# The transform over the sequence in an attention, Fourier and MLP kernel: nine products over all outputs, or even and odd rows apart for half of them

## The chip, the cores and the metric

One Trainium2 chip; the kernel runs on one of its cores. Times are microseconds on the device; the time of a kernel is the median of its runs. Engines are named as in the profile: PE (matmuls; PEld is its weight load), DVE (vector), ACT (scalar), POOL (GpSimd), SP (which issues the DMAs).

## The reference

Three stages run one after the other on 4 batches of 576 rows and 512 features.

```
out_up    = repeat(softmax_attention(mean4(q), mean4(k), mean4(v)), 4)   # over groups of 4 rows
out_local = softmax_attention(q, k, v, only where |i - j| < 4)
x = out_up + out_local                                # [4, 576, 512], 8 heads of 64

mixed = real(fft(fft(x, over the 576 rows), over the 512 features))
u = x + mixed
ch = relu(layernorm(u) @ w_ch1) @ w_ch2               # 512 -> 2048 -> 512
x = u + ch

gate = sigmoid(causal depthwise convolution of x, 5 taps)
out = (gate * (x @ w_val)) @ w_out
```

The part at issue is `mixed`. The real part of the two Fourier transforms is a product with cosines over features and rows less a product with sines over both. Outputs m and 576 - m of the transform over the rows differ by the sign of the sine part alone, so 289 outputs of each part are computed (m = 0 to 288).

## The kernel before, in words

**Layout.** `X` of a batch holds 4 x 128 features on partitions and the 576 rows along the free dimension. All of `attn_steps(b)` (from L428) works on one batch: the local and the low-resolution attention, then the transform, which adds `mixed` to `X` in place. What follows works on units of 192 rows (`UT`), three a batch, twelve in all: `ln` (L1009) normalizes a unit, `mlp_steps` (L1133; `steps32`, L1095, for the first unit, in fp32) has the two big products, `moe2_steps` (L1189) the gated stage. Large products in fp16 are made of three matmuls each: both operands are split into a high and a low fp16 part, and the product of the low parts is left out.

**The transform of a batch** has these steps, from L842 on:

- *Folding* (L857 to L880): for c = 0, 1 (feature halves) and sd = 0, 1, DVE (POOL for sd = 1 of batches 1 to 3) makes `fs`, DVE makes `fF` by adding and subtracting row t and row 576 - t (289 rows kept, two parities e), ACT rounds it to `FH` in fp16 (L876), and DVE makes the rest `FL` (L877).
- *Transform over the features* (L891 to L917; L845 to L855 in batch 0, where it runs piece by piece after each fold): `TT` cuts the 289 rows into groups of 97, 96 and 96. The rows of a group are the weights' columns (`lhsT`), the moving operand is 127 to 129 columns of the table `feat`; 72 matmuls a batch fill `ab` in PSUM. ACT rounds it to `AH`, DVE makes `AL`, with the group's rows on partitions and 514 features along the free dimension.
- *Transform over the rows* (`seq_mm`, L919; `sums0`, L929, has the same loop for batch 0): for each c, `pp` (cosines) and `pq` (sines) are sums over the three groups and three fp16 passes: nine matmuls with 128 columns of `AH` or `AL` as weights and 289 columns of the table `seq` moving. `pn` is the same for the one feature 256 left over, with one column of weights. That makes five products a batch.
- *Sums* (L943 to L960; L970 to L987 for batches 1 to 3): ACT copies `pq` times a scale to `qs`; DVE makes `DS[:, 0]` = scaled `pp` - `qs` and `DS[:, 1]` = scaled `pp` + `qs`, the outputs 0 to 288 and those mirrored. ACT overwrites row 0 of `DS` of c = 0 with `pn`. Eight additions put `DS` on the two halves of `X`: 289 rows read forward, 287 read backward (`HALF - 2:0:-1`). For batches 1 to 3 the backward ones run on POOL. In batch 0 four of the eight read a mirrored copy in PSUM (`mir`).

`qs`, `DS`, `fs`, `fF` and other tiles of this kind share one ring of three buffers (tag "E" of `prp`). `pp`, `pq`, `pn` and `ab` share two banks of PSUM (tag "t", L35 to L39).

**Weights.** `w_ch1`, `w_ch2`, `w_val` and `w_out` come as 64-bit words; DVE makes fp32 of them by integer operations (`to_f32`, L303) in ring buffers, which the next loads reuse.

**Order.** The program is a list of events with positions in units of MLP stages: `spread` (L1371) puts a batch's steps between two positions (`P_D`, `P_E`, `S_F0`), `urgent` (L176) raises a step's priority (the transform has key "F"). Within that, the compiler of the kernel orders the instructions of each engine by priority and by a model of their costs, worked out anew at every build, gives out buffers of the rings and adds the waits; on the chip each engine runs its list strictly in order.

Of the kernel before, what the change touches and what calls it, by code (L numbers as in the profile page):

```python
# [25 lines left out]
HALF = S // 2 + 1  # L26
TT = ((0, 97), (97, 96), (193, 96))
SCALE = 0.125
# [67 lines left out]
def constants():  # L96
# [12 lines left out]
    wt[0] = wt[-1] = 0.5  # L109
    seq = np.zeros((97, 2, 3, 2, HALF))  # L110
    for j, m in enumerate((np.cos(ang) * wt, np.sin(ang) * (wt == 1.0))):
        for i, (n0, n) in enumerate(TT):
            seq[:n, j, i, 0] = m[n0:n0 + n]
    h, lo = split16(seq[:, :, :, 0])
    seq = np.stack([h, lo], 3)
    p, c = np.arange(128)[:, None], np.arange(128)[None, :]
# [6 lines left out]
        "c_feat": np.ascontiguousarray(feat.reshape(128, 2048)),  # L123
        "c_seq": np.ascontiguousarray(seq.reshape(97, 12 * HALF)),
        "c_band": (np.concatenate([band.reshape(128, 4 * WK), eye], 1).view(np.int32) >> 16).astype(np.int16),
# [5 lines left out]
def attn_moe_kernel(ctx, tc, q_t, k_t, v_t, w1, w2, w_val, conv_t, w_out, c_feat, c_seq, c_band, c_eye, out):  # L131
# [91 lines left out]
    def load_consts2():  # L223
        load(out=craw, in_=conv_t)
        load(out=feat, in_=c_feat.rearrange("p (a b c) -> p a b c", a=2, b=2))
        load(out=seq, in_=c_seq.rearrange("p (a b c d) -> p a b c d", a=2, b=3, c=2))

# [200 lines left out]
    def attn_steps(b):  # L428
# [414 lines left out]
        abs_ = []  # L843

        def piece(c, sd):  # L845
            if not abs_:
                abs_.extend(pst(x, [97, 512]) for x in ("ab", "ab", "eT"))
            for i, (n0, n) in enumerate(TT):
# [41 lines left out]

        for i, (n0, n) in enumerate(TT):  # L891
            def f(i=i, n0=n0, n=n):
                ps = abs_[i] if b == 0 else pst("ab", [97, 512])
                for (c0, c1), sd, e in () if b == 0 else [(FC[z], z % 2, z // 2) for z in range(4)]:
                    t = 0
                    for c in range(2):
                        for x, w in (("FH", 0), ("FH", 1), ("FL", 0)):
                            T.matmul(  # L898
                                out=ps[0:n, c0:c1], lhsT=d[x][:, c, sd, e, n0:n0 + n],
                                rhs=feat[:, w, c, c0:c1], start=(t == 0), stop=(t == 5),  # L900
                            )
                            t += 1
# [16 lines left out]
        def seq_mm(ps, col, m, j):  # L919
            t = 0  # L920
            for i, (n0, n) in enumerate(TT):
                for x, w in (("AH", 0), ("AH", 1), ("AL", 0)):
                    d["seqed"] = T.matmul(
                        out=ps, lhsT=d[x][0:n, i, col:col + m], rhs=seq[0:n, j, i, w, :],
                        start=(t == 0), stop=(t == 8),
                    )
                    t += 1

        def sums0():  # L929

# [24 lines left out]
            for e in (1, 0):  # L955
                A.activation(out=DSs[0][0:1, e], in_=pn, func=AF.Copy, scale=d["ivx8"][0:1, 0:1])
# [7 lines left out]
        for c in range(2 if b else 0):  # L964
            def f(c=c):
                pp = pst("pp", [P, HALF])
                seq_mm(pp, 128 * c, 128, 0)
                pq = pst("pq", [P, HALF])
                seq_mm(pq, 258 + 128 * c, 128, 1)
                qs = prp.tile([P, HALF], F32, tag="E", name="qs", bufs=3)  # L970
                iv = d["ivx8"][:, 0:1]
                A.activation(out=qs, in_=pq, func=AF.Copy, scale=iv)
                DS = prp.tile([P, 2, HALF], F32, tag="E", name="DS", bufs=3)
                stt(V, DS[:, 0], pp, iv, qs, ALU.mult, ALU.subtract)
                i = stt(V, DS[:, 1], pp, iv, qs, ALU.mult, ALU.add)
                X = d["X"]
# [506 lines left out]
```

## Time and profile before

| | |
|---|---|
| median of 3 runs | 725.42 us (724.97 to 728.31) |
| the profiled execution | 727.02 us |
| its span in the profile | 725.2 us |
| mean granted clock of PE, of full speed | 0.971 |

The span is the time from the profile's first to its last instruction; the rest of the execution's own time (1.8 us) lies around it. The clock of PE is at its full level outside 20 to 60 us and a stretch near 260 us. In the profile a matmul's busy time runs to its modelled end, and matmuls overlap; their pace is read from the chain of work or from their starts.

### The profile page before, as it was taken

Reading aid. Unit: us, or ns where it says so; the run is one execution under the profiler, and the core shown is the slowest. Engines: PE = TensorE matmul, PEld = TensorE weight load, DVE = VectorE, ACT = ScalarE, POOL = GpSimd, SP = SyncE. Lnnn points to the kernel's source line nnn. Section 1 sums busy time; section 2 is a strip of 40 time slices with the busy share of each in tenths; the row PEclk is TensorE's granted clock in tenths of the full one; section 3 lists DMA queues with packets and bytes.
Section 4 is the critical chain, followed back from the end, with each engine's and each line's share of the span. In section 5 each row is a group of like instructions: output and inputs, shape, how many; then the busy total and the mean of one; then the engine's idle time right before and its main releaser. Section 6 shows DMA issues by size and latency. Waiting matters only on the chain.

```text
span 725.2 us, 18322 instructions
## 1 busy us (share of the span) xinstructions
PE 680.2 (94%) x7785; PEld 591.6 (82%) x7785; DVE 462.7 (64%) x975; ACT 327.1 (45%) x999; POOL 118.6 (16%) x167
## 2 busy tenths in 40 slices
PE   8498798999989969999999999999999999999997
PEld 4265598898888749787998898798899989999895
DVE  4669699969885796628677625739535672723324
ACT  3574273796423465656434644834323232222222
POOL 2200012431120252330211316003100010000000
PEclk9659999999999989999999999999999999999999
DMA  8975352531435001240130001002000000000001
GB/s 243 295 285 177 117 208 67 140 126 33 145 99 154 17 2 36 99 116 17 45 120 3 20 21 43 16 12 89 15 17 15 2 16 16 2 16 2 31 1 45
DMA packets 27574, 53.01 MB, mean 73 GB/s; under 512 B 2112, under 2 KB 16320, under 8 KB 26468
## 3 DMA queue, kind: packets, MB, share of 16 engines
q1 hardware_dynamic: 27492, 51.84, 22.8%
q8 instruction: 61, 1.00, 0.6%
q14 instruction: 21, 0.17, 0.1%
HBM read 45.34 MB, written 8.26 MB: 74 GB/s over the span
## 4 chain that ended last, share of the span: by engine, by line
PE 62%; DVE 20%; DMA 9%; ACT 4%; POOL 2%; issue 2%; SPq 1%; ACTq 0%; DVEq 0%; POOLq 0%
PE pc L1166 18%; PE ph L1146 17%; DVE W L168 8%; PE out L1274 6%; PE val L1258 4%; DMA vw<-in_v_dram 2%; PE po L785 2%; PE pc L1121 2%; DMA v<-in_v_dram 2%; PE dO L617 2%; DMA raw<-in_moe_w_out_dram 1%; PE ab L898 1%; PE sc L734 1%; DVE qkT L628 1%; PE eT L775 1%
## 5 line engine op out<-in xcount | busy, mean ns | idle before, releaser
L1146 PE MATMUL ph<-uh,W 128*128 128x192 f16 x1408 | 197.0, 247 | 1.4 <-ACT uh L1072 1.4
L1146 PEld LDWEIGHTS <-W 128*128 128x128 f16 x2112 | 176.4, 98 | 10.3 <-issue 7.6
L1146 PE MATMUL ph<-ul,W 128*128 128x192 f16 x704 | 173.8, 247 | 0.0
L1166 PE MATMUL pc<-hh,W 128*128 128x192 f16 x1232 | 171.1, 246 | 0.0
L1166 PEld LDWEIGHTS <-W 128*128 128x128 f16 x1848 | 153.5, 98 | 5.5 <-issue 4.1
L1166 PE MATMUL pc<-hl,W 128*128 128x192 f16 x616 | 150.6, 246 | 1.3 <-DVE hl L168 1.3
L168 DVE SCALAR_TENSOR_TENSOR hl<-ph,hh 128x384 f16<-128x384 f32 x88 | 48.5, 552 | 90.5 <-ACT hh L1150 90.3
L1150 ACT ACTIVATE hh<-ph 128x384 f16<-128x384 f32 x88 | 43.1, 489 | 102.4 <-PE ph L1146 97.6
L168 DVE SCALAR_TENSOR_TENSOR W<-X,cw,W 128x192 f32<-128x192 f32 x160 | 60.7, 433 | 0.5 <-ACT W L1221 0.2
L1258 PE MATMUL val<-yy,W 128*128 128x192 f16 x576 | 53.2, 246 | 2.3 <-DVE yy L168 2.0
L1258 PEld LDWEIGHTS <-W 128*128 128x128 f16 x576 | 48.1, 98 | 4.4 <-issue 2.6
L576 ACT ACTIVATE dP<-dS,dmx 128x64 f32<-128x64 f32 x160 | 48.0, 333 | 3.3 <-PE dPT L597 2.6
L1274 PE MATMUL out<-W,gh 128*128 128x512 f16 x144 | 46.6, 386 | 0.9 <-ACT gh L1265 0.9
L576 ACT ACTIVATION_READ_ACCUMULATOR dP<-dS,dmx 128x1 f32 x160 | 36.2, 227 | 0.0
L1274 PE MATMUL out<-W,gl 128*128 128x512 f16 x72 | 27.8, 386 | 2.2 <-DVE gl L168 2.2
L168 DVE SCALAR_TENSOR_TENSOR W<-W,W 128x1024 int32<-128x1024 int32 x24 | 28.3, 1216 | 0.1
L1274 PEld LDWEIGHTS <-gh 128*128 128x128 f16 x144 | 14.2, 99 | 15.2 <-issue 1.0
L1166 PEld LDWEIGHTS <-Wz 128*128 128x128 f16 x264 | 22.2, 98 | 5.2 <-issue 2.8
L749 ACT ACTIVATE E<-sc,nm 72x144 f32<-72x144 f32 x64 | 23.5, 375 | 4.0 <-POOL vr L174 3.2
L1221 ACT ACTIVATE W<-X,cw 128x192 f32<-128x192 f32 x40 | 15.6, 449 | 20.6 <-DVE X L168 20.3
L1166 PE MATMUL pc<-hh,Wz 128*128 128x192 f16 x176 | 24.7, 246 | 0.0
L1121 PE MATMUL pc<-h,W 128*128 128x192 f32 x128 | 23.0, 330 | 1.8 <-DVE tr L171 1.2
(246 smaller groups left out, 1203.2 us busy)
## 6 DMA issues: line engine op xcount, KB each, us to landing
W<-in_moe_w_ch_dram SPq DMA_DIRECT2D x12, 1024.0 KB
v<-in_v_dram SPq DMA_DIRECT2D x32, 144.0 KB
out_dram<-osb SPq DMA_DIRECT2D x17, 256.0 KB
vw<-in_v_dram SPq DMA_DIRECT2D x16, 256.0 KB
X<-in_q_dram SPq DMA_DIRECT2D x6, 576.0 KB
kT<-in_k_dram SPq DMA_DIRECT2D x4, 582.0 KB
X<-in_moe_w_ch_dram SPq DMA_DIRECT2D x2, 1024.0 KB
raw<-in_moe_w_ch_dram SPq DMA_DIRECT2D x4, 512.0 KB
```

Source lines behind the costliest of these rows:

```text
L168: return eng.scalar_tensor_tensor(out=out, in0=in0, scalar=scalar, in1=in1, op0=op0, op1=op1)
L576: A.activation(out=s_[:, z, a], in_=pss[par][:, z, a], func=AF.Exp, scale=SCALE, bias=mx[:, par, z, a:a + 1], accum_out=su[:, par, z, a:a ...
L617: d["dO"] = T.matmul(out=pos[x][par * 64:par * 64 + 64, a2, o:o + nq], lhsT=vw[g][row, 2 * z + hf, c:c + D], rhs=pts[z][row, par, a2, hf * ...
L749: A.activation(out=E[:, qc], in_=ps[:, qc], func=AF.Exp, scale=SCALE / 16, bias=nm[:, qc:qc + 1], accum_out=su[:, qc:qc + 1],)
L785: T.matmul(out=po[par * 64:par * 64 + 64], lhsT=d["vr"][:, kc, (a % 2) * 4 + (a // 2) * 2 + par], rhs=ets[par][:, kc], start=(kc == 0), st ...
L1121: T.matmul(out=c["ps"][m // 2][:, m % 2], lhsT=W[9 + g][:, o:o + 128], rhs=hs[g // 2][:, g % 2, e, :], start=(kk == 0 and m % 2 == 0), sto ...
L1146: T.matmul(out=ps[:, e], lhsT=w1_ap(pw, kc, 2 * g + e), rhs=uh[px][:, kc, :], start=(t == 0), stop=(t == 11))
L1150: A.activation(out=h_, in_=ps, func=AF.Relu)
L1166: T.matmul(out=ps[m // 2][:, m % 2], lhsT=w2_ap(pw, kk, m), rhs=x[px][:, e, :], start=(kk == 0 and (pw, px) == (0, 0) and m % 2 == 0), sto ...
L1221: A.activation(out=m, in_=x, func=AF.Copy, scale=w)
L1258: T.matmul(out=ps[:, e], lhsT=wv_ap(pw, kc, 2 * mh + e), rhs=m_["y"][px][:, kc, :], start=(t == 0), stop=(t == 11))
L1274: T.matmul(out=ps, lhsT=(gh, gl)[px][:, kc, t * 128:(t + 1) * 128], rhs=wo_ap(pw, kc), start=(n == 0), stop=(n == 11))
```

## The change

With m[k] the table of cosines or sines, m at output 288 - j equals m at output j for even rows k (cosine) and its negative for odd ones; for the sines it is the other way round. So the sum over even rows and the sum over odd rows are made apart for outputs 0 to 144 only (`HP` = 145), and their sum and difference give all 289.

- `TT` now groups the 289 rows as 128 even rows of the first 256, 128 odd ones, and the last 33. `rows_of` picks them out of `FH` and `FL`: every second column for the first two groups.
- `seq` holds 145 columns for each of the first two groups and 2 x 145 for the third, where even rows have zeros in the odd half and odd rows in the even half. The third group's three matmuls write both halves of `pp` at once (290 columns), the others one half (145).
- `sums` makes `R` (for both signs, the even and the odd part) where `qs` and `DS` were made, and `fold` makes `DS` from `R` with one addition and one reversed subtraction. `nyquist` copies `pn` to row 0 of `R` and folds that row again.
- In `sums0` the additions keep their places; `nyquist` comes after the second addition to `X[:, 0]`.

```diff
-TT = ((0, 97), (97, 96), (193, 96))
+HP = HALF // 2 + 1
+TT = (128, 128, HALF - 256)
+PAR = ((0, 0, HP), (1, HP, HP), (slice(None), 2 * HP, 2 * HP))
...
-    seq = const.tile([97, 2, 3, 2, HALF], F16, name="seq")
+    seq = const.tile([P, 2, 2, 4 * HP], F16, name="seq")
...
+        def rows_of(x, c, sd, e, i):
+            f = d[x][:, c, sd, e]
+            return f[:, i:256:2] if i < 2 else f[:, 256:HALF]
...
-                            out=abs_[i][0:n, c0:c1], lhsT=d[x][:, c, sd, e, n0:n0 + n], rhs=feat[:, w, c, c0:c1],
+                            out=abs_[i][0:n, c0:c1], lhsT=rows_of(x, c, sd, e, i), rhs=feat[:, w, c, c0:c1],
...
         def seq_mm(ps, col, m, j):
             t = 0
-            for i, (n0, n) in enumerate(TT):
+            for (o, k0, nk), (i, n) in zip(PAR, enumerate(TT)):
                 for x, w in (("AH", 0), ("AH", 1), ("AL", 0)):
                     d["seqed"] = T.matmul(
-                        out=ps, lhsT=d[x][0:n, i, col:col + m], rhs=seq[0:n, j, i, w, :],
+                        out=ps[:, o], lhsT=d[x][0:n, i, col:col + m], rhs=seq[0:n, j, w, k0:k0 + nk],
                         start=(t == 0), stop=(t == 8),
                     )
                     t += 1
+        def fold(DS, R):
+            add(V, DS[:, :, 0:HP], R[:, :, 0], R[:, :, 1])
+            V.tensor_tensor(out=DS[:, :, HALF - 1:HP - 1:-1], in0=R[:, ::-1, 0, 0:HP - 1], in1=R[:, ::-1, 1, 0:HP - 1],
+                            op=ALU.subtract)
+
+        def sums(pp, pq):
+            iv = d["ivx8"][:, 0:1]
+            R = prp.tile([P, 2, 2, HP], F32, tag="E", name="R", bufs=3)
+            A.activation(out=R[:, 1], in_=pq, func=AF.Copy, scale=iv)
+            DS = prp.tile([P, 2, HALF], F32, tag="E", name="DS", bufs=3)
+            stt(V, R[:, 0], pp, iv, R[:, 1], ALU.mult, ALU.subtract)
+            stt(V, R[:, 1], pp, iv, R[:, 1], ALU.mult, ALU.add)
+            fold(DS, R)
+            return DS, R
+
+        def nyquist(DS, R):
+            pn = pst("pn", [1, 2, HP])
+            seq_mm(pn, 256, 1, 0)
+            for e in (1, 0):
+                A.activation(out=R[0:1, e], in_=pn, func=AF.Copy, scale=d["ivx8"][0:1, 0:1])
+            fold(DS[0:1], R[0:1])
...
-                pp = pst("pp", [P, HALF])
+                pp = pst("pp", [P, 2, HP])
                 seq_mm(pp, 128 * c, 128, 0)
-                pq = pst("pq", [P, HALF])
+                pq = pst("pq", [P, 2, HP])
                 seq_mm(pq, 258 + 128 * c, 128, 1)
-                qs = prp.tile([P, HALF], F32, tag="E", name="qs", bufs=3)
-                iv = d["ivx8"][:, 0:1]
-                A.activation(out=qs, in_=pq, func=AF.Copy, scale=iv)
-                DS = prp.tile([P, 2, HALF], F32, tag="E", name="DS", bufs=3)
-                stt(V, DS[:, 0], pp, iv, qs, ALU.mult, ALU.subtract)
-                i = stt(V, DS[:, 1], pp, iv, qs, ALU.mult, ALU.add)
+                DS, R = sums(pp, pq)
...
                 if c == 0:
-                    pn = pst("pn", [1, HALF])
-                    seq_mm(pn, 256, 1, 0)
-                    for e in range(2):
-                        A.activation(out=DS[0:1, e], in_=pn, func=AF.Copy, scale=d["ivx8"][0:1, 0:1])
+                    nyquist(DS, R)
```

## Rows read from the trace of the kernel before

**Rows 1.** The page, part 1: busy us (share of the span) and instructions of each engine

```profile
PE 680.2 (94%) x7785; PEld 591.6 (82%) x7785; DVE 462.7 (64%) x975; ACT 327.1 (45%) x999; POOL 118.6 (16%) x167
```

**Rows 2.** Busy by stretch: length, PE, PEld, DVE, ACT, POOL (instructions), clock, DMA

```profile
120.00:140.00 20.00, 16.92 (x237) 15.41 (x228) 19.72 (x29) 11.42 (x42) 3.42 (x4) 1.00 0.59 150
...
520.00:540.00 20.00, 20.00 (x209) 17.40 (x208) 7.80 (x15) 4.51 (x9) 3.11 (x4) 1.00 0.04 14
```

**Rows 3.** The chain of waits in order of time: start us, us, engine, tile, line, count

```profile
374.91 1.35 PE ab L898 x24
...
380.36 1.12 PE pq L923 x9
...
422.89 1.98 PE ph L1146 x24
```

**Rows 4.** Weight loads by line and shape (busy us, mean ns), and a stretch of the chain

```profile
L898 PEld LDWEIGHTS <-FH 128*96 128x96 f16 x96 | 8.4, 124 | 0.0
...
L365 PEld LDWEIGHTS <-W 128*128 128x128 bf16 x80 | 5.3, 97 | 3.6 <-DVE W L168 2.5 <-issue 0.6
...
245.48 0.52 PE cv L365 x9
```

**Rows 5.** DVE's instructions by line and shape, and two rows of the timeline at 242 us

```profile
L870 DVE TENSOR_TENSOR fF<-fs 128x289 f32<-128x289 f32 x32 | 13.7, 470 | 0.2
...
242.09 1.66 POOL L174 TENSOR_TENSOR X<-X,DS 128x287 f32<-128x287 f32 x2 [2.92 <-DVE DS L168]
...
242.28 1.78 DVE L174 TENSOR_TENSOR X<-X,DS 128x289 f32<-128x289 f32 x2
```

**Rows 6.** Timeline of batch 0's sums; in brackets the idle time before and its releaser

```profile
82.97 0.94 DVE L168 SCALAR_TENSOR_TENSOR DS<-pp,ivx,qs 128x289 f32<-128x289 f32 x2 [2.46 <-ACT qs L944]
...
85.98 0.41 PE L923 MATMUL pn<-seq,AH 97*1 97x289 f16 x2 [0.27 <-ACT qs L944]
...
87.30 0.88 ACT L956 ACTIVATE DS<-pn,ivx 1x289 f32<-1x289 f32 x2 [1.37 <-DVE X L174]
...
88.29 0.81 DVE L174 TENSOR_TENSOR X<-mir,DS 128x289 f32<-128x289 f32 x2
...
89.75 0.96 DVE L1031 TENSOR_TENSOR u<-X,st 128x768 f32<-128x768 f32 x1 [0.65 <-PE st L1019]
```

**Rows 7.** The chain of waits, batch 0's products and what follows

```profile
80.15 1.12 PE pp L941 x9
...
85.43 0.51 ACT qs L944
...
140.95 6.77 PE pc L1121 x40
```

**Rows 8.** The chain of waits, batch 1

```profile
226.78 1.36 PE ab L898 x24
...
228.51 6.57 DMA kT<-in_k_dram
...
236.38 0.95 DVE DS L168 x2
...
251.52 0.37 PE st L1025 x2
```

**Rows 9.** Timeline of DVE and PE, batch 2

```profile
389.48 0.94 DVE L168 SCALAR_TENSOR_TENSOR DS<-pp,ivx,qs 128x289 f32<-128x289 f32 x2 [2.79 <-ACT qs L972]
...
396.16 0.55 DVE L168 SCALAR_TENSOR_TENSOR hl<-ph,hh 128x384 f16<-128x384 f32 x1
...
396.76 0.24 PE L1166 MATMUL pc<-hl,Wz 128*128 128x192 f16 x1 [1.19 <-DVE hl L168]
```

**Rows 10.** Timeline of DVE, batch 3

```profile
527.44 0.94 DVE L168 SCALAR_TENSOR_TENSOR DS<-pp,ivx,qs 128x289 f32<-128x289 f32 x2 [2.68 <-ACT qs L972]
```

**Rows 11.** Readers and writer of the table `seq`: duration ns, first and last start us

```profile
L941 PE MATMUL pp<-seq,AH x12: 283/288/289, 80.0 to 83.9; 96*128 96x289 f16 x8, 97*128 97x289 f16 x4
...
L189 SPq DMA_DIRECT2D seq<-in_c_seq_dram x1: 250/250/250, 35.3 to 35.3; - x1
```

More of the change, by code (lines that the diff above doesn't have):

```diff
@@ L109, in constants @@
     wt[0] = wt[-1] = 0.5
-    seq = np.zeros((97, 2, 3, 2, HALF))
+    seq = np.zeros((128, 2, 4 * HP))
     for j, m in enumerate((np.cos(ang) * wt, np.sin(ang) * (wt == 1.0))):
-        for i, (n0, n) in enumerate(TT):
-            seq[:n, j, i, 0] = m[n0:n0 + n]
-    h, lo = split16(seq[:, :, :, 0])
-    seq = np.stack([h, lo], 3)
+        m = m[:, :HP]
+        seq[:, j, 0:HP] = m[0:256:2]
+        seq[:, j, HP:2 * HP] = m[1:256:2]
+        seq[0:HALF - 256:2, j, 2 * HP:3 * HP] = m[256::2]
+        seq[1:HALF - 256:2, j, 3 * HP:] = m[257::2]
+    h, lo = split16(seq)
+    seq = np.stack([h, lo], 2)
     p, c = np.arange(128)[:, None], np.arange(128)[None, :]
@@ L123, in constants @@
         "c_feat": np.ascontiguousarray(feat.reshape(128, 2048)),
-        "c_seq": np.ascontiguousarray(seq.reshape(97, 12 * HALF)),
+        "c_seq": np.ascontiguousarray(seq.reshape(128, 16 * HP)),
         "c_band": (np.concatenate([band.reshape(128, 4 * WK), eye], 1).view(np.int32) >> 16).astype(np.int16),
@@ L225, in load_consts2 @@
         load(out=feat, in_=c_feat.rearrange("p (a b c) -> p a b c", a=2, b=2))
-        load(out=seq, in_=c_seq.rearrange("p (a b c d) -> p a b c d", a=2, b=3, c=2))
+        load(out=seq, in_=c_seq.rearrange("p (a b c) -> p a b c", a=2, b=2))
     def warm(i):
@@ L843, in attn_steps @@
         abs_ = []
+        def rows_of(x, c, sd, e, i):
+            f = d[x][:, c, sd, e]
+            return f[:, i:256:2] if i < 2 else f[:, 256:HALF]
         def piece(c, sd):
             if not abs_:
-                abs_.extend(pst(x, [97, 512]) for x in ("ab", "ab", "eT"))
-            for i, (n0, n) in enumerate(TT):
+                abs_.extend(pst(x, [P, 512]) for x in ("ab", "ab", "eT"))
+            for i, n in enumerate(TT):
                 for e in range(2):
@@ L889, in _, with f @@
             d["AL"] = acc_t("AL", [P, 3, 514], F16)
-        for i, (n0, n) in enumerate(TT):
-            def f(i=i, n0=n0, n=n):
-                ps = abs_[i] if b == 0 else pst("ab", [97, 512])
+        for i, n in enumerate(TT):
+            def f(i=i, n=n):
+                ps = abs_[i] if b == 0 else pst("ab", [P, 512])
                 for (c0, c1), sd, e in () if b == 0 else [(FC[z], z % 2, z // 2) for z in range(4)]:
@@ L898, in f @@
                             T.matmul(
-                                out=ps[0:n, c0:c1], lhsT=d[x][:, c, sd, e, n0:n0 + n],
+                                out=ps[0:n, c0:c1], lhsT=rows_of(x, c, sd, e, i),
                                 rhs=feat[:, w, c, c0:c1], start=(t == 0), stop=(t == 5),
@@ L927, in seq_mm @@
                     t += 1
+        def fold(DS, R):
[17 more added lines that the diff above has]
+            fold(DS[0:1], R[0:1])
         def sums0():
-            X, iv = d["X"], d["ivx8"][:, 0:1]
+            X = d["X"]
             a0, a1, b0, b1 = PAD, PAD + HALF, PAD + HALF, PAD + S
@@ L934, in sums0 @@
             for c in range(2):
-                pp = pst("pp", [P, HALF])
-                pq = pst("pq", [P, HALF])
+                pp = pst("pp", [P, 2, HP])
+                pq = pst("pq", [P, 2, HP])
                 t = 0
-                for i, (n0, n) in enumerate(TT):
+                for (o, k0, nk), (i, n) in zip(PAR, enumerate(TT)):
                     for ps, col, j in ((pp, 128 * c, 0), (pq, 258 + 128 * c, 1)):
                         for q, (x, w) in enumerate((("AH", 0), ("AH", 1), ("AL", 0))):
-                            T.matmul(out=ps, lhsT=d[x][0:n, i, col:col + 128], rhs=seq[0:n, j, i, w, :],
+                            T.matmul(out=ps[:, o], lhsT=d[x][0:n, i, col:col + 128], rhs=seq[0:n, j, w, k0:k0 + nk],
                                      start=(i == 0 and q == 0), stop=(i == 2 and q == 2))
-                qs = prp.tile([P, HALF], F32, tag="E", name="qs", bufs=3)
-                A.activation(out=qs, in_=pq, func=AF.Copy, scale=iv)
-                DS = prp.tile([P, 2, HALF], F32, tag="E", name="DS", bufs=3)
-                stt(V, DS[:, 0], pp, iv, qs, ALU.mult, ALU.subtract)
-                i = stt(V, DS[:, 1], pp, iv, qs, ALU.mult, ALU.add)
+                DS, R = sums(pp, pq)
+                if c == 0:
+                    R0 = R
                 add(V, X[:, c, a0:a1], X[:, c, a0:a1], DS[:, 0])
@@ L951, in sums0 @@
             warm_after(add(V, X[:, 3, a0:a1], m[1][0], DSs[1][:, 1]), 2)
-            pn = pst("pn", [1, HALF])
-            seq_mm(pn, 256, 1, 0)
             add(V, X[:, 0, b0:b1], X[:, 0, b0:b1], DSs[0][:, 1, HALF - 2:0:-1])
-            for e in (1, 0):
-                A.activation(out=DSs[0][0:1, e], in_=pn, func=AF.Copy, scale=d["ivx8"][0:1, 0:1])
+            nyquist(DSs[0], R0)
             warm_after(add(V, X[:, 1, b0:b1], X[:, 1, b0:b1], DSs[1][:, 1, HALF - 2:0:-1]), 2)
@@ L965, in f @@
             def f(c=c):
-                pp = pst("pp", [P, HALF])
+                pp = pst("pp", [P, 2, HP])
                 seq_mm(pp, 128 * c, 128, 0)
-                pq = pst("pq", [P, HALF])
+                pq = pst("pq", [P, 2, HP])
                 seq_mm(pq, 258 + 128 * c, 128, 1)
-                qs = prp.tile([P, HALF], F32, tag="E", name="qs", bufs=3)
-                iv = d["ivx8"][:, 0:1]
[L972 to L975, printed above, removed]
+                DS, R = sums(pp, pq)
                 X = d["X"]
```

3 lines of the change are left out of this document (removed).

## The prediction

> **What bounds the kernel now.** I read the page first, then the busy time by stretch, then the chain that ended last, and only then single instructions. The page shows PE busy for 94% of the span and DVE for 64% [rows 1]; the stretches show that this average hides two regimes. At 520 to 540 us PE is full (20.00 us of 20) and DVE works 7.80, while between 120 and 140 us DVE is the full one (19.72 of 20) [rows 2]. So an instruction more on DVE is dear early and nearly free late, and a column less on PE is worth its time only late. The change touches both engines in all four batches: batch 0's copy of this stage lies at 80 to 90 us, ahead of DVE's full stretch, the others near 236, 385 and 527 us [rows 6, 8 to 10].
>
> **PE, removed.** A product of the stage (`seq_mm`) is nine matmuls of 289 columns and takes 1.12 us, 124 ns each [rows 3]. In the new form six of the nine have 145 columns and three 290. No matmul of 145 columns with a full weight load is in the trace; its neighbours are 24 of 128 columns in 1.35 us, 56 ns each, and 24 of 192 in 1.98 us, 82.5 ns each [rows 3], which lie on a line of 0.41 ns a column, and that line meets the 124 ns at 289. On it 145 columns cost 63 ns: 6 x (124 - 63) = 0.37 us a product, and five products (two `pp`, two `pq`, one `pn`) make 1.84 us a batch. Bounds: 56 ns and 82.5 ns, so 2.0 to 1.25 us a batch; I take 63 because the three rows agree on the line.
> A rule speaks against this. The rows have each matmul paired with a weight load of its own and still spaced at 56 ns for 128 columns [rows 3]. The Trainium skill, "TensorE: Matmul & The Clock Gate", section "Back-to-back issue gap", gives about 81 ns for such pairs at 128 columns and 131 at 512, as the weight load needs its share. Read between these figures, an estimate from that page, a short matmul would save only about 18 ns and a batch 0.6 us. The trace disagrees, so the sum stays with the rows.
>
> **Weights with a step of two.** The step before (L898; L852 in batch 0) now loads every second column of `FH`/`FL`. Before, a load of 96 columns takes 124 ns; a load of 128 columns takes 97 ns, and that row (L365) already reads every second element. Its stream of nine matmuls takes 0.52 us, 58 ns each, against 56 [rows 4]. 48 loads of a batch are of this kind: 48 x 2 ns = 0.1 us; the third row group (33 columns) keeps its spacing under 128 moving columns. Cost zero to 0.1 us, covered by nothing where PE is full.
>
> **DVE, added.** `qs` (289 elements) becomes `R[:, 1]` (290) on ACT and the two scale-and-combine instructions stay, as do the eight additions to `X` and the two ACT copies of the last row. New are six instructions a batch, two for each `fold`: c = 0, c = 1, and row 0 again in `nyquist`. Their nearest rows are fp32 additions of 289 elements with one operand reversed, 13.7 us for 32, 0.43 us each [rows 5]; I give the pair on a single partition the same. Sum 2.5 us a batch. The dear bound is the addition that runs beside POOL, 1.78 us for two while POOL adds to the other half of `X` [rows 5]: 0.89 us each, 5.3 a batch. I take 0.41, what batch 0's additions cost without POOL [rows 6], since only `nyquist`'s pair runs beside POOL.
>
> **Batch 0.** Here PE's products lie on the chain: `pp` and `pq` of c = 0, ACT's `qs`, the same for c = 1 (its `qs` ends at 85.94), then DVE [rows 7]. Four products save 1.47 us of it, two of them before DVE's first `DS`, which comes at 82.24 in place of 82.97 [rows 6]. From there DVE has the 4.8 us that it works now (four combinations at 0.47, eight additions at 0.41 to 0.45) and 2.5 more, so without any hole it ends at 89.5, against 89.10 now (88.29 + 0.81) [rows 6]. There is a hole: `R`, `DS`, `R`, `DS` need four buffers of a ring of three, so the second `DS` waits until `nyquist` has used the first `R`. After the second `qs` (84.47) come `pn` (0.75 us, and 0.2 to drain: its copies now begin 1.32 us after it starts, for 1.12 us of matmuls [rows 6]), two ACT copies (0.88) and the fold of row 0, so DVE waits from 85.76 to about 86.3. End 90.05: a loss of 1.0 us. Cheap bound 0.0, if the additions that the first LN needs go first; dear bound 2.2, if none of `pn` and its copies (1.83 us) is covered. Behind it the chain is DVE's: LN's subtraction at 89.75 [rows 6], then the words of the weights and the loads that these release, until PE takes the chain over at 140.95 with the second MLP product [rows 7]. So the 1.0 us reaches the stages after it.
>
> **Batch 1.** The stage waits for `kT`'s load, 228.5 to 235.1, which starts when the step before it has read `FH`/`FL`; only then DVE, in order, gets from the reduction behind that load to `DS` [rows 8]. What PE saves before 235 is gone. After it `pp` and `pq` of c = 1 save 0.73 us up to the LN sums that POOL waits for at 252 [rows 8]; DVE's fold of c = 1 (2 x 0.41) lies beside PE's MLP work there. Gain 0.5 us, bounds 1.8 and a loss of 0.9 (both remaining folds uncovered less the 0.73).
>
> **Batch 2.** The chain is PE's up to 389, so the five products give 1.84 us. Then a heap of DVE work sets the end: `DS` at 389.48, additions, taps, until `hl` at 396.16, for which PE stands still 1.19 us [rows 9]. The fold of c = 1 joins that heap: 0.82 back. Gain 1.0, bounds 1.84 and a loss of 0.6 (all three folds in the heap).
>
> **Batch 3.** PE is full [rows 2] and DVE waits 2.68 us for `qs` [rows 10], so its folds are covered: gain 1.8, bounds 1.84 and 1.0. If that cover went, `hl` would be late next.
>
> The table of the sequence transform shrinks from 657 KB to 128 x 16 x 145 x 2 bytes = 580 KB. Its load is issued at 35 us and first read at 80 [rows 11]: nothing.
>
> **Sum.** +1.0 - 0.5 - 1.0 - 1.8 = -2.3 us. The profiled execution took 727.02 us with a span of 725.2, the three runs have a median of 725.42; I set the sum against the median: 723.1. The bounds added up give -5.4 to +2.7.
>
> **The rivals.** *DVE covers everything* (720.3). If batch 0's additions are put in the cheap order and batches 1 and 2 keep their folds off the chain, three batches give 1.7 us each and batch 0 nothing: -5.1. For it: DVE is idle in a third of the span [rows 1]. Against: the heap at 390 us and the ring in batch 0.
> *The folds lengthen DVE's chain* (728.1). Place: batch 0's ring and the heap of batch 2. It decides if the second `fold` finds DVE without other work while `pn` goes through PE and ACT, +2.2, and if batches 1 and 2 pay their dear bounds, +0.9 and +0.6, against 1.0 left in batch 3: +2.7. The order of all instructions is worked out anew from modelled costs when the kernel is built, and a neighbour that moves can add one or two waits such as the 1.19 us of [rows 9], to 730. For it: DVE at 19.72 of 20. Against: two of the four stages have DVE holes.
> *The short matmuls are no shorter* (728.7). If loads set the pace, so that matmuls of 145 and of 128 columns with the new loads come every 82.5 ns, PE gains 1.25 us a batch and gives 48 x 26 ns = 1.25 back. Batch 0 then loses 1.0 + 1.47 and batch 2 its fold, 0.8: +3.3. The 58 ns of [rows 4] speak against it. The gap rule of the Trainium skill's page on TensorE, cited above, is this mechanism.
>
> **How the numbers follow.** Forecast 0.48, DVE covers everything 0.29, longer chain 0.18, no shorter matmuls 0.05. A measurement here can tell about 0.5% (3.6 us) from no change: faster means under 721.8, slower over 729.0. The second case lies under 721.8 except for a tenth, and a seventh of the forecast spills over it by reordering: 0.33 faster. Of the third case two thirds pass 729.0 by such waits, with 0.03 of the others: 0.15 slower; 0.52 within. The range, 718.8 to 729.2, holds the forecast, the second case with a neighbour that moves well, and the third at its own price; beyond it lie reordered forms of both. As cases of both signs count, the forecast's own range is 721 to 725.5.
>
> **What would show it.** `seq_mm` groups with 145 columns spaced near 63 ns and a product in 0.75 us; weight loads of L898's successor at about 97 ns; six new fp32 instructions a batch of 0.4 us; in batch 0 a DVE wait for the ACT copies of `pn` before the second `DS`, and LN's subtraction about 1 us later than 89.75; batches 2 and 3 each shorter. I am wrong if the products do not shrink, if LN's subtraction comes earlier than now, or if batch 3's stretch is no shorter.

## The result, and the profile after

The kernel after takes 734.67 us (median of 4 runs, 734.22 to 737.23), the kernel before beside it 725.19 (724.46 to 728.31): a ratio of 1.0132, interval 1.0105 to 1.0158. It is 9.5 us slower where the forecast was 2.3 us faster, and outside the range.

The page of the kernel after, part 1, answers to [rows 1]; its profiled execution took 737.23 us with a span of 735.4:

```profile
PE 689.1 (94%) x7785; PEld 592.6 (81%) x7785; DVE 473.0 (64%) x999; ACT 326.6 (44%) x999; POOL 120.9 (16%) x167
```

PE has fewer columns to stream and is busy 8.9 us longer: busy time at a lower clock counts in full, and so do the gaps inside a group of matmuls. The next fence is PE's timeline of one `pq` of batch 1, start and length:

```profile
249.86 0.29 PE L932 MATMUL pq<-seq,AH 128*128 128x145 f16 x2
249.99 0.22 PE L932 MATMUL pq<-seq,AL 128*128 128x145 f16 x1
250.05 0.29 PE L932 MATMUL pq<-seq,AH 128*128 128x145 f16 x2
250.18 0.23 PE L932 MATMUL pq<-seq,AL 128*128 128x145 f16 x1
250.34 0.42 PE L932 MATMUL pq<-seq,AH 33*128 33x290 f16 x2
250.60 0.28 PE L932 MATMUL pq<-seq,AL 33*128 33x290 f16 x1
250.81 0.34 PE L1164 MATMUL ph<-uh,W 128*128 128x192 f16 x2
```

Read the starts. From 249.86 to 250.18 lie five steps of 64 ns: the short matmuls cost what was forecast. But the step from 128 rows of weights to 33 takes 0.16 us, some 94 ns more, and the step back 0.21 in place of 0.12. The product needs 0.95 us until the next work starts, against 1.12 before [rows 3] and the 0.75 forecast. The 24 matmuls of a group of the step before show the same at a change from 128 columns of weights to 33, 1.46 us in place of 1.35; the first fence is the chain, the second the weight loads by shape (busy us, mean ns), which hold 98 ns, as forecast from [rows 4]:

```profile
236.74 1.46 PE ab L907 x24
```

```profile
L907 PEld LDWEIGHTS <-FH 128*128 128x128 f16 x96 | 6.9, 98 | 3.2 <-ACT FH L885 3.0
...
L907 PEld LDWEIGHTS <-FH 128*33 128x33 f16 x48 | 3.6, 98 | 0.5 <-issue 0.3 <-DVE AL L173 0.2
```

Batch 0, DVE's timeline, answers to [rows 6]:

```profile
85.40 0.83 DVE L179 TENSOR_TENSOR X<-X,DS 128x289 f32<-128x289 f32 x2
86.81 1.07 DVE L173 SCALAR_TENSOR_TENSOR R<-pp,ivx,R 128x290 f32<-128x290 f32 x2 [0.58 <-ACT R L946]
89.75 0.45 DVE L179 TENSOR_TENSOR DS<-R 1x290 f32<-1x290 f32 x1 [1.87 <-ACT R L957]
...
90.60 0.46 DVE L179 TENSOR_TENSOR DS<-R 128x290 f32<-128x290 f32 x1
...
94.92 0.95 DVE L1049 TENSOR_TENSOR u<-X,st 128x768 f32<-128x768 f32 x1 [1.28 <-PE st L1037]
```

The hole is where the prediction put it: the second fold waits for the row's, and that for ACT's copies of `pn`. It lasts 1.87 us, not 0.5, and LN's subtraction comes at 94.92, 5.2 us later than 89.75 [rows 6]; it also waits 1.28 us for the column sums `st`, 0.65 before [rows 6]. In the stretches (length, PE, PEld, DVE, ACT, POOL, clock, DMA) and on the chain one more thing is seen. The first fence is the kernel after by stretch, the second the same stretch of the kernel before, the third the chain of the kernel after:

```profile
82.00:84.00 2.00, 1.41 (x16) 0.92 (x14) 0.54 (x2) 0.50 (x1) 0.00 (x0) 1.00 0.04 8
84.00:86.00 2.00, 1.91 (x12) 1.03 (x12) 1.93 (x5) 0.00 (x0) 0.00 (x0) 0.65 0.00 0
...
90.00:92.00 2.00, 0.00 (x0) 0.00 (x0) 1.97 (x6) 0.00 (x0) 0.00 (x0) 0.50 0.00 0
```

```profile
82.00:84.00 2.00, 1.41 (x13) 0.97 (x11) 1.03 (x3) 0.50 (x1) 0.00 (x0) 1.00 0.17 61
```

```profile
84.55 1.69 PE pq L972 x9
87.17 1.65 PE pn L932 x9
```

The granted clock falls from 1.00 to 0.50, from the 2.4 to the 1.2 GHz level, behind a stretch in which PE stands idle for some 0.6 us; the second `pq` and `pn` run in it and take 1.7 us each. The kernel before stands idle for the same 0.6 us at that place (1.41 us busy of 2) and stays at 1.00, so this idle time does not explain the fall by itself, and what else it took is not shown.

Batch 3, DVE's timeline, answers to [rows 10]: the wait for ACT is still there, and longer, so the folds lie in cover.

```profile
538.76 1.08 DVE L173 SCALAR_TENSOR_TENSOR R<-pp,ivx,R 128x290 f32<-128x290 f32 x2 [3.40 <-ACT R L946]
```

**Where the time went, by stretch.** Five stretches can be cut at the same instructions in every kernel, by starts on ScalarE's timeline: T0 from batch 0's first `FH` to the first `sq` (70.9 to 90.8 us before), T1 to the third `sq` (172.4), T2 to the third `uh` (264.2), T3 to batch 3's first `FH` (490.5), T4 to the tenth `sq` (567.1). T0 holds batch 0's transforms, T2 batch 1's, T3 batch 2's, T4 batch 3's; the 158 us behind T4 are alike in all kernels. Lengths in us, one profiled execution each, beside the median of the runs:

| kernel | median | T0 | T1 | T2 | T3 | T4 |
|---|---|---|---|---|---|---|
| before | 725.19 | 19.9 | 81.6 | 91.8 | 226.3 | 76.6 |
| after | 734.67 | 25.2 | 85.6 | 93.8 | 226.1 | 76.0 |
| e1 regrouping alone | 729.98 | 21.5 | 81.9 | 92.5 | 227.1 | 77.9 |
| e2 passes alone | 735.41 | 22.2 | 84.4 | 92.8 | 230.1 | 76.6 |
| e3 after, 65 rows | 731.92 | 22.4 | 85.8 | 93.1 | 227.4 | 74.7 |
| e4 after, row tile | 726.98 | 23.1 | 81.9 | 92.7 | 223.2 | 76.0 |
| e5 both mends | 724.37 | 21.6 | 80.2 | 92.4 | 222.8 | 74.7 |
| e13 passes, batch 0 | 732.74 | 21.9 | 85.0 | 92.5 | 229.5 | 76.6 |
| e14 passes, later | 726.52 | 19.9 | 82.1 | 91.9 | 226.4 | 76.5 |
| e15 before, order of after | 729.52 | 20.5 | 83.4 | 94.2 | 224.4 | 76.6 |
| e16 after, order of before | 731.11 | 25.2 | 81.7 | 90.3 | 229.4 | 76.0 |
| e17 e13, order of before | 727.14 | 22.1 | 81.7 | 91.5 | 226.7 | 76.6 |
| e18 e5, order of before | 726.01 | 21.6 | 81.7 | 91.5 | 225.3 | 74.7 |

T4 repeats to 0.1 us between kernels with the same matmuls. T1 to T3 differ between two executions of one kernel by more: the executions of before lie between 722 and 729 us. After against before: T0 +5.3, T1 +4.0, T2 +2.0, T3 -0.2, T4 -0.6. (The two profiled executions are 10.2 us apart, the medians 9.5.)

### The profile page after: what moved, and what is told of

It is laid out like the page before. It is cut to its first block, busy times and chain, and to the rows that moved or that the text cites. A ratio compares the mean times of both kernels' runs of the same rounds, so it can differ in the third digit from the quotient of the medians.

```text
span 735.4 us, 18343 instructions
## 1 busy us (share of the span) xinstructions
PE 689.1 (94%) x7785; PEld 592.6 (81%) x7785; DVE 473.0 (64%) x999; ACT 326.6 (44%) x999; POOL 120.9 (16%) x167
## 3 DMA queue, kind: packets, MB, share of 16 engines
q1 hardware_dynamic: 27538, 51.76, 22.1%
## 4 chain that ended last, share of the span: by engine, by line
PE 63%; DVE 18%; DMA 9%; POOL 4%; ACT 3%; issue 2%; SPq 1%; DVEq 0%; ACTq 0%; POOLq 0%
PE pc L1184 19%; PE ph L1164 18%; DVE W L173 8%; PE out L1292 7%; PE val L1276 4%; DMA v<-in_v_dram 3%; DMA vw<-in_v_dram 2%; DMA raw<-in_moe_w_out_dram 2%; PE sc L739 2%; PE po L790 2%; PE ab L907 1%; DVE W L311 1%; DVE fF L879 1%; PE eT L780 1%; DVE X L179 1%
## 5 line engine op out<-in xcount | busy, mean ns | idle before, releaser
L173 DVE SCALAR_TENSOR_TENSOR hl<-ph,hh 128x384 f16<-128x384 f32 x88 | 48.6, 553 | 91.1 <-ACT hh L1168 90.8
L1292 PE MATMUL out<-W,gl 128*128 128x512 f16 x72 | 27.8, 386 | 1.6 <-DVE gl L173 1.6
L1126 PE MATMUL ph<-u,W 128*128 128x192 f32 x128 | 25.8, 358 | 1.0 <-DVE u L1049 1.0
L1184 PE MATMUL pc<-hh,Wz 128*128 128x192 f16 x176 | 26.5, 256 | 0.0
L780 PE MATMUL eT<-eye,E 72*72 72x72 f32 x128 | 17.5, 251 | 8.9 <-POOL E L176 4.5
```

Of the source, the lines that this page charges most:

```text
L173: return eng.scalar_tensor_tensor(out=out, in0=in0, scalar=scalar, in1=in1, op0=op0, op1=op1)
L780: T.transpose(out=pe[:, kc, qc], in_=lr[par][:, qc, kc * QC:(kc + 1) * QC], identity=eye[0:QC, 0:QC],)
L1126: i = T.matmul(out=ps[:, e], lhsT=W[AT[kc * 2 + m // 8] + 1][:, o:o + 128], rhs=u()[:, kc, :], start=(kc == 0), stop=(kc == 3))
L1184: T.matmul(out=ps[m // 2][:, m % 2], lhsT=w2_ap(pw, kk, m), rhs=x[px][:, e, :], start=(kk == 0 and (pw, px) == (0, 0) and m % 2 == 0), sto ...
L1292: T.matmul(out=ps, lhsT=(gh, gl)[px][:, kc, t * 128:(t + 1) * 128], rhs=wo_ap(pw, kc), start=(n == 0), stop=(n == 11))
```

## The experiments

**What the shapes cost: e1 and e3.** e1 gives the kernel before the new row groups alone (outputs 289 wide, no folds), e3 gives the kernel after a third group of 65 rows, for the first 32 of which the table holds zeros.

```diff
-TT = ((0, 97), (97, 96), (193, 96))
+TT = ((0, 128), (1, 128), (256, 33))
...
-lhsT=d[x][:, c, sd, e, n0:n0 + n]
+lhsT=rows_of(x, c, sd, e, i)
```

> The kernel before with the regrouping alone: groups of 128 even rows, 128 odd rows and 33 last rows in place of 97, 96 and 96, all outputs still 289 columns wide, no folding. Theory M (a change between 128 and 33 rows or columns of weights costs TensorE about 94 ns each way): a product of nine takes about 1.30 us in place of 1.12, the 33-column group of 24 takes 1.45 in place of 1.35, so 12 changes, 1.1 us a batch, about 4 us in all: 729 us. Theory of the prediction (the shape of the weights costs nothing): 1.12 and 1.35 us, 725.2 us.

```diff
-TT = (128, 128, HALF - 256)
+TT = (128, 128, 65)
...
-        return f[:, i:256:2] if i < 2 else f[:, 256:HALF]
+        return f[:, i:256:2] if i < 2 else f[:, HALF - 65:HALF]
```

> The kernel after with a third group of 65 rows (224 to 288, the table zero for the first 32 of them) in place of 33. Theory M: no more gaps at the change of group; a product takes 0.75 us in place of 0.85 to 0.97, an ab stage 1.35 in place of 1.45, about 1.1 us a batch and more in batch 0: 730 us, and the later batches alone gain some 3.4 us. Rival (the gap comes from the third group's width of 290 columns or from its place in the sum): products stay at 0.85, time 734 to 735 us.

e1: 729.98 us, ratio 1.0070 (1.0043 to 1.0097). On its chain a `pq` of nine takes 1.22 us in place of 1.12 (the step back from 33 rows falls into the row behind it), a `pn` 1.30 in place of 1.21, and a group of 24 1.46 in place of 1.35:

```profile
227.63 1.46 PE ab L902 x24
...
233.28 1.22 PE pq L927 x9
```

e3: 731.92 us, 2.8 less than the kernel after and 2 more than theory M gave. Its timeline of a `pq`:

```profile
247.76 0.23 PE L932 MATMUL pq<-seq,AL 128*128 128x145 f16 x1
247.82 0.41 PE L932 MATMUL pq<-seq,AH 65*128 65x290 f16 x2
248.07 0.29 PE L932 MATMUL pq<-seq,AL 65*128 65x290 f16 x1
248.19 0.33 PE L1164 MATMUL ph<-uh,W 128*128 128x192 f16 x2
```

With 65 rows the steps in and out are 0.06 and 0.12 us: the gaps are gone, though the group does more work. T4 gives the sum to 0.1 us, since PE is full there: regrouping +1.3, the whole change -0.6, the change with 65 rows -1.9, the passes 0.0. The 1.8 us that the prediction counted for a batch are there; the gaps take 1.3 of them. Theory M holds: about 94 ns each way for 33 against 128, none for 65. The Trainium skill, "TensorEngine Tiling (Array Packing)", section "Key Properties", says that changing the tiling mode drains the TensorE; its section "Available Configurations" lists modes of 128, 64 and 32 rows. These runs fit that if weights of 33 rows are run in a smaller mode than those of 65, which the page does not say and no run here shows.

**The ring: e4, and both mends: e5.**

```diff
             pn = pst("pn", [1, 2, HP])
             seq_mm(pn, 256, 1, 0)
+            RN = prp.tile([1, 2, 2, HP], F32, tag="RN", name="RN", bufs=1)
             for e in (1, 0):
-                A.activation(out=R[0:1, e], in_=pn, ...)
-            fold(DS[0:1], R[0:1])
+                A.activation(out=RN[0:1, e], in_=pn, ...)
+            fold(DS[0:1], RN)
```

> The kernel after with a tile of its own for the single row, so that the second fold of batch 0 no longer waits for the first tile R. Theory R (the ring of three buffers is the loss of batch 0): the fold of the second half starts at about 88 us, not at 90.6, u is done at about 92 in place of 94.9, total about 731 us. Theory K (the granted clock at 0.50 from 84.6 us on makes it, whatever the ring): u at 93 to 94 us, total 733 to 734 us.

> Both mends on the kernel after: the single row's own tile and a third group of 65 rows. Theory of two separate losses (the ring in batch 0 and the gaps at each change between 128 and 33 rows or columns): 727.0 less the 2 to 3 us that the 65 rows took off alone, 724 to 725 us, and the span of the three later batches 3 us shorter than with the row tile alone. Rival (what the row tile gave came from the order that followed, by luck): 728 us or more again.

e4: 726.98 us (1.0028, 1.0002 to 1.0055), 7.7 less than the kernel after, more than either theory gave. DVE's timeline shows the second fold ahead of the row's:

```profile
86.98 1.07 DVE L173 SCALAR_TENSOR_TENSOR R<-pp,ivx,R 128x290 f32<-128x290 f32 x2
88.09 0.46 DVE L179 TENSOR_TENSOR DS<-R 128x290 f32<-128x290 f32 x1
88.47 0.45 DVE L940 TENSOR_TENSOR DS<-R 128x288 f32<-128x288 f32 x1
89.22 0.45 DVE L179 TENSOR_TENSOR DS<-RN 1x290 f32<-1x290 f32 x1 [0.30 <-ACT RN L958]
```

The hole is 0.30 us, but T0 is only 2.1 us shorter than in the kernel after; the rest of the gain lies in T1 to T3, where the row tile has little to do. e5: 724.37 us, ratio 0.9973 (0.9956 to 0.9990), the one version that beats the kernel before clear of noise.

**What the folds cost: e2, e13, e14.** The sum tile is taken as the maximum of itself and itself, in the sizes of the folds: the same VectorE time with no other change of the work. e13 and e14 do it in batch 0 alone and in the later batches alone.

```diff
+        def again(DS):
+            for c0, c1 in ((0, 145), (145, HALF)):
+                V.tensor_tensor(out=DS[:, :, c0:c1], in0=DS[:, :, c0:c1], in1=DS[:, :, c0:c1], op=ALU.max)
```

> The kernel before with six more VectorE instructions a batch alone (the sum tile taken as the maximum of itself and itself, in place, in the two sizes of the folds; for the single row too). Theory F (the folds lengthen VectorE's chain in every batch): about 2.5 us in batch 0 and 1 to 2 us in each later one, 730 us or more. Theory B (what the change loses is lost in batch 0 alone, by the order and the clock): at most the 1 to 2.2 us of batch 0, 726 to 727.5 us.

> The kernel before with the six VectorE passes in batch 0 alone. Theory A (a delay of about 2 us in batch 0 is all it takes: it is carried on, and the list of instructions laid out from it is another one and worse): u about 2 us late, the stretch from 118 to 172 us another 2 to 3 us longer, 730 us or more. Theory L (the passes of the later batches cost by themselves): the 2 us of batch 0 and no more, 727 to 728 us.

> The kernel before with the six VectorE passes in batches 1 to 3 alone. Theory L: most of the 10 us that the passes cost in all four batches, the stretch of batch 2 (359 to 446 us) 5 us longer as with all of them, 730 us or more. Theory A: 725 to 727 us.

735.41, 732.74 and 726.52 us; ratios 1.0128 (1.0093 to 1.0164), 1.0087 (1.0057 to 1.0117) and 1.0022 (0.9999 to 1.0046). Eighteen passes in three batches cost a microsecond, six in batch 0 cost seven, though T0 itself is only 2.0 us longer by them. The rest lies in T1 (+3.4) and T3 (+3.2), in which e13 has the very same work as before.

**A detour: POOL's scaling of `E`: e6, e7, e9 to e12.** POOL scales the tiles `E` of batch 1's softmax by the reciprocal of their sums, `lsu`. In T1 of the kernel after, PE waits for this. First the kernel before, then the kernel after (POOL's timeline, and the table of waits: in total, times, longest):

```profile
158.78 0.66 POOL L171 TENSOR_TENSOR E<-E,lsu 72x288 f32<-72x288 f32 x1 [7.94 <-PE sc L734]
161.00 0.66 POOL L171 TENSOR_TENSOR E<-E,lsu 72x288 f32<-72x288 f32 x1 [1.56 <-DVE lsu L754]
```

```profile
165.13 5.70 POOL L176 TENSOR_TENSOR E<-E,lsu 72x288 f32<-72x288 f32 x2 [7.92 <-DVE lsu L758]
```

```profile
PE eT L780 <- POOL E L176: 4.0, 2, 2.9
```

I first moved the work to ScalarE (`EN_G = (1,)` becomes `EN_G = ()`), in the kernel after and, as control, in the kernel before.

> The kernel after with the scaling of batch 1's tiles E on ScalarE in place of POOL, nothing else. Theory P (at 165 to 171 us two of POOL's instructions take 2.03 and 3.59 us beside VectorE in place of 0.66, and TensorE waits 4 us for them and then runs at a granted clock of 0.5): 4 to 5 us less, about 730 us. Theory O (the loss there is the later order alone): 734 to 735 us, with as long a wait for ScalarE instead.

> The kernel before with the same edit, the control: POOL's two instructions take 0.66 us each there and TensorE does not wait for them, so theory P gives no gain, 725 us, or a us or two more for ScalarE's longer queue. If this gains 4 us too, the edit is good by itself and tells nothing of the change.

746.54 us, and 727.76 for the control (1.0014, 0.9994 to 1.0034). This told nothing: the order of all instructions changed with it, and T2 of e6 grew to 101.0 us by new waits (5.9 us for `yy`, 5.2 for `FL`). One place that differs just ahead of the wait is VectorE's reciprocal of `E`'s sums: it stands ahead of both additions of unit 0's product to X in before, behind the first in after. An ordering edge, without a wait, swaps it:

```diff
+                if z == 0:
+                    tc.add_manual_dep(st[0]["inverse"], i.ins.name, ...)
```

> The kernel before, with one VectorE instruction in another place of its queue: the reciprocal (72x2) for batch 1's first tile E stands behind the first addition of unit 0's product to X (PSUM and SBUF) instead of ahead of both. Theory P (POOL's scaling of E, 0.66 us, is held up wherever VectorE reads two operands from SBUF; after the swap the conversion of W follows 0.5 us behind the reciprocal and catches it): POOL's two instructions take 2 us and more in place of 0.66, TensorE waits some 3 us for E at 161 to 165 us, the granted clock falls behind it, and the kernel before is 3 to 5 us slower, 729 to 730 us, without any part of the change. Theory O (the order of these is without effect, the delay comes from what the change does elsewhere): 725.5 us.

> The kernel after with the same instruction put back ahead of both additions, as the kernel before has it. Theory P: POOL's two instructions take 0.66 us each again, TensorE does not wait for E, and 4 to 5 us come back: 730 us; what stays is batch 0's 5 us and the gaps at the changes of group, less what the shorter products give. Theory O: 734 to 735 us.

> The kernel before with the six VectorE passes a batch, and the same instruction put back. Theory P: 3 to 4 us less than the 735.4 of the passes alone, 731 to 732 us. Theory F (the passes themselves are what costs): 735 us.

> The kernel with both mends (724.4 us), with the reciprocal put behind the first addition. Theory P: TensorE's wait for E comes back and with it 3 to 5 us, 728 to 729 us. Theory O: 724.4 us.

The lever works. In e9 (DVE's timeline, POOL's, the waits):

```profile
160.42 0.15 DVE L754 RECIPROCAL lsu<-lsu 72x2 f32<-72x2 f32 x1
160.49 0.53 DVE L174 TENSOR_TENSOR X<-pc,X 128x384 f32<-128x384 f32 x1
160.94 1.27 DVE L168 SCALAR_TENSOR_TENSOR W<-W,s_w,W 128x1024 f16<-128x1024 f32 x1
...
162.92 1.27 DVE L168 SCALAR_TENSOR_TENSOR W<-W,s_w,W 128x1024 f16<-128x1024 f32 x1
164.12 1.39 DVE L168 SCALAR_TENSOR_TENSOR tap<-X,cw,tap 128x192 f32<-128x192 f32 x4
165.43 0.41 DVE L306 TENSOR_SCALAR W<-raw 128x512 int32<-128x512 int32 x1
165.77 0.55 DVE L168 SCALAR_TENSOR_TENSOR hl<-ph,hh 128x384 f16<-128x384 f32 x1
```

```profile
160.74 5.63 POOL L171 TENSOR_TENSOR E<-E,lsu 72x288 f32<-72x288 f32 x2 [8.42 <-DVE lsu L754]
```

```profile
PE eT L777 <- POOL E L171: 2.0, 2, 1.7
```

POOL's second scaling ends at 166.37 (160.74 + 5.63), 0.6 us after DVE turns to `hl`, whose operand `ph` lies in PSUM; while DVE goes through `W` and `tap`, with both operands in SBUF, POOL hardly gets on. And in e10 the two scalings take 0.66 us each again. But the totals hardly move: e9 725.88 beside 725.44 (1.0009, 0.9991 to 1.0026), e10 733.89, e11 736.44, e12 725.41 (0.9998, 0.9978 to 1.0017). Against their unswapped forms that is +0.4, -0.8, +1.0 and +1.0 us, where theory P gave 3 to 5. In e11 the scalings are back at 0.66 us each, so it should have gained; the sign is the wrong one. In T1 the swap costs e9 2.0 us (83.6), and T2 gives 2.5 back. So the wait is real and worth about a microsecond at most; theory P falls as the main cause. The Trainium skill, "SBUF — State Buffer", section "Who interferes with whom", says that a VectorE instruction with two SBUF inputs contends with a GpSimd instruction that reads SBUF; the traces agree, with 5.63 us for the two scalings in e9 beside 1.32 in the kernel before.

**The clock: e8.** Three more products keep PE busy behind the second fold, in e5.

```diff
+            for e in range(2):
+                T.matmul(out=ps[:, 0:HALF], lhsT=ones, rhs=DSs[1][:, e], start=True, stop=True)
...
             nyquist(DSs[0], R0)
+            T.matmul(out=ps[:, 0:HALF], lhsT=ones, rhs=DSs[0][:, 1], start=True, stop=True)
```

> The kernel with both mends, and three idle products on TensorE in batch 0 that wait for the second fold and for the row's fold, to keep the engine busy while VectorE adds. Theory K (the gap of 2 to 3 us before the column sums lets the granted clock fall to 0.5 for some 10 us, and the single-precision products that follow then take twice as long): granted clock 1.00 from 89 to 100 us, 3 to 4 us less than with both mends alone, about 721 us. Rival: the clock stays up and the time does not move, because VectorE's work sets that stretch, 724 to 725 us.

735.11 us, 10.7 more than e5. The first fence is e8 by stretch, the second e5:

```profile
92.00:94.00 2.00, 1.10 (x7) 0.81 (x5) 0.86 (x1) 0.00 (x0) 0.00 (x0) 1.00 0.00 0
```

```profile
92.00:94.00 2.00, 0.95 (x4) 0.93 (x4) 1.94 (x3) 0.95 (x2) 0.00 (x0) 0.50 0.00 0
```

The clock is back at 1.00 by 92 us, and nothing is won: T0 is 1.0 us longer (22.6), and from the first `sq` to the first `uh` e8 takes 27.6 us, e5 27.8 with its first part at half clock, the kernel before 27.7. So theory K falls from the first `sq` on. Ahead of it the matter stays open: LN's subtraction waits 1.38 us for the column sums in e5 at half clock, 0.65 in before [rows 6], and in e8, where the added products stand ahead of those sums, 2.74. The 10 us were lost in T1 (95.7 us), where the order was yet another and PE waited 6.5 us for POOL's `E`.

**The order: e15 to e18.** The kernel after, e2, e3 and e13 are longer in batch 0 and lose time in T1 too, where none of their added work lies; e4 and e5 are longer in batch 0 as well, by 3.2 and 1.7 us, and lose nothing over T1 to T3. The order of the instructions on each engine is laid out when the kernel is built, from modelled times. These four hold one kernel's work in another's order: all instructions of PE, DVE, ACT and POOL, in program order, are chained by ordering edges in the sequence that the other kernel's queue has; the folds or passes, which have no counterpart, go where they fit. The edges add no waits of their own; buffers and waits follow from the order, as in every build.

```diff
+    for key in "VAGT":
+        row = made[key]
+        at = order[o:o + len(row)]
+        o += len(row)
+        for x, y in zip(at, at[1:]):
+            tc.add_manual_dep(row[y], row[x].name, ...)
```

> The kernel before, all its work unchanged, its instructions on TensorE, VectorE, ScalarE and POOL laid out in the order that the kernel after has. Theory O (the order is what costs most): a good part of the 9.5 us, 730 us or more, lost in the stretches behind batch 0 (118 to 172 us above all), the batch 0 itself at its 19.9 us. Theory D (a delay of 2 to 5 us in batch 0 is what costs, through work that has to wait for it): 725 to 726 us.

> The kernel after with its instructions laid out in the order of the kernel before, the folds wherever they fit. Theory O: what is lost is batch 0's 5 us at most, and the later batches give some 2 us back, 727 to 729 us. Theory D: 734 to 735 us.

> The kernel before with the six VectorE passes in batch 0 alone, all else in its own order. Theory O: 725.5 plus the 2 us of batch 0, 727 to 728 us, in place of 732.7. Theory D: 732 to 733 us as before.

> The kernel with both mends in the order of the kernel before. Theory O: its order by its own is as lucky as that of before, so about the same 724 us, or 2 us less where the stretch of 91 to 172 us is as in before; batch 0 still 1.7 us longer, each later batch 1.9 us shorter: 721 to 724 us. Theory D: 724.4 us as it is.

e15: 729.52 us, 1.0041 (1.0019 to 1.0063). The kernel before, with none of the change's work, is 3.4 us slower in the other order (726.17 beside it), and brings PE's wait for `E` along:

```profile
159.59 5.71 POOL L166 TENSOR_TENSOR E<-E,lsu 72x288 f32<-72x288 f32 x2 [9.04 <-PE ph L166]
```

```profile
PE eT L166 <- POOL E L166: 3.4, 2, 3.0
```

e16: 731.11 us, 1.0064 (1.0043 to 1.0085), 3.6 less than in its own order, or 4.5 with each set against the kernel before beside it; T0 is 25.2 as in its own order, T1 81.7 and POOL's scaling at its 0.66 us:

```profile
164.00 0.66 POOL L171 TENSOR_TENSOR E<-E,lsu 72x288 f32<-72x288 f32 x1 [7.84 <-PE sc L171]
166.22 0.66 POOL L171 TENSOR_TENSOR E<-E,lsu 72x288 f32<-72x288 f32 x1 [1.56 <-DVE lsu L171]
```

e17: 727.14 us (1.0012, 0.9993 to 1.0032) in place of 732.74: six passes in batch 0 cost 1.0 us in the old order (726.17 beside it) and 7.2 in their own (725.52 beside it). e18: 726.01 (1.0003, 0.9986 to 1.0021), 1.6 more than e5 in its own order (1.0 with each beside its own before) and 2 above what theory O gave: an order can also be a lucky one. Theory O holds for the part behind batch 0; e16 came out 2 us above its expectation, since T3 was 3 us longer there. In e18, in the same order, T3 is no longer than in before, so that is not the order's; its cause stays open.

## Why the prediction was wrong

The loss of 9.5 us has two parts of known size: batch 0's transforms, +5.3 us in T0, in either order (after and e16); and the order, 3.4 us (e15) to 4.5 (e16, each beside its own before). What is left, -0.4 to 0.8 us, is all that the later batches come to, where the sum had -0.5, -1.0 and -1.8. T1 to T3 repeat too badly between executions to split it further.

- **Short matmuls, 63 ns**: right (64). **"Four products save 1.47 us", "1.84 us a batch"**: failed, as a product's 0.37 us became 0.17 (1.12 - 0.95). The step that failed is "the third row group (33 columns) keeps its spacing": inside the group it does, at its edges each change costs some 94 ns; for the product of nine the sum had no term for a change of rows at all. With 65 rows T4 was 1.9 us shorter, the 1.84 of the prediction. The price could be read in the trace of the kernel before, at `pn`, whose weights have one column and which the sum took at 1.12 us like the rest. PE's timeline of batch 2 there:

```profile
383.47 0.25 PE L1166 MATMUL pc<-hl,W 128*128 128x192 f16 x1
383.64 0.41 PE L923 MATMUL pn<-seq,AH 97*1 97x289 f16 x2
...
384.64 0.28 PE L923 MATMUL pn<-seq,AL 96*1 96x289 f16 x1
384.86 0.34 PE L1166 MATMUL pc<-hh,W 128*128 128x192 f16 x2
```

The step into one column takes 0.17 us in place of the 0.08 of a matmul of 192 columns, the step back 0.22 in place of 0.12; `pn` takes 1.21 us on the chain there, `pq` 1.12 [rows 3].
- **Weights with a step of two**: right, 98 ns a load, no cost to be seen.
- **DVE's folds**: a bit over, 0.46 and 0.45 us against 0.41; the pair on one partition costs as much as on 128, as assumed. **Batch 3's cover**: right, the passes cost nothing in T4.
- **Batch 0, +1.0, dear bound 2.2**: failed, 5.3. By the runs: 2.0 to 2.3 us for the folds (e13, e17, e2), 1.5 to 1.6 for the gaps (e4 to e5, e1) and 0.8 for the ring (e3 to e5), against 0.3 to 0.6 that the short products give (e5 at 21.6 beside 21.9 to 22.2 for passes alone). In e1, e3, e4 and e5 the clock was 1.00 through these products. The kernel after is another 1.3 us longer than the sum of these, which came only with gaps and ring together and, in after, e10 and e16 alike, with the half clock; what the clock alone costs there is not separated. The hole was named and priced at 0.5; it measured 1.87 to 2.29 us (after, e10, e16), as the short path through `pn` ran with the gaps and at half clock, and 1.09 in e3, without the gaps and at full clock. The bound was drawn at full clock.
- **"So the 1.0 us reaches the stages after it"**: a delay is carried, but that was not the larger part. e17 has the delay without the new order and loses 1.0 us. The prediction knew that the order is worked out anew, and priced it, as "one or two waits", in one rival only. It is a term of its own, of either sign: 6 us in e13 (7.2 against the 1.0 of e17), and a gain of 1.0 in e5 (beside e18).
- **The rivals**: the third case, longer DVE chain, had the right sign and the right place in batch 0, and the wrong one in batch 2 (e14: passes in the later batches, 1.0 us in all). The fourth, no shorter matmuls, was wrong in its mechanism; another limit of the weights' shape took two thirds of batch 3's gain (1.9 to 0.6).
- **"I am wrong if"**: none of the three signs came. Products shrank, LN's subtraction came later, T4 is 0.6 us shorter, and the forecast was wrong all the same.
- **The later batches**: with the gaps mended and the old order (e18), T2, T3 and T4 are 0.3, 1.0 and 1.9 us shorter than before, near the forecast 0.5, 1.0 and 1.8. T2 and T3 are from one execution each, so part of that can be luck.
- **The bounds**: the lower ones add up to -5.5, not -5.4; nothing hangs on it.

Not settled: which of the moved neighbours makes the 3.4 to 4.5 us, and what besides idle time lets the clock fall in batch 0. The one that could be moved alone, the reciprocal, is worth about 1.

## What to carry to other kernels

Split a contraction so that its pieces do not change the shape of the weights in a way that costs a step: 65 rows, 32 of them zeros, were cheaper than 33. Look for such steps in the old trace first, at any product with narrow weights. Where a planner lays out the order, an edit early in the kernel is two edits, its work and a new order; hold the old order by edges, and the new work's price can be measured by itself. A temporary that a late step still needs should not sit in a ring from which the next one's buffer comes.

## What was not expected of the hardware

- Between weights of 128 rows or columns and of 33, each change costs TensorE about 94 ns (after, e1), and so does one between 128 columns and one (before); between 128 and 65, 96 or 97 none was seen (e3, before).
- Two POOL scalings of 72x288 took 5.63 to 5.71 us in place of 1.32 while VectorE worked on SBUF operands (after, e9, e15).
- The granted clock fell to 0.50 in batch 0 of the kernel after, behind idle time that before has too and stays at 1.00. Between the first `sq` and the first `uh` that cost no time: 27.7 us in before at 1.00 throughout, 27.7 in the kernel after with part of it at 0.50.
